# Attention and two expert layers on one core: q and k turned and summed in one product, batch 0's v summed on the tensor engine, and a new table of places

## The chip, the cores and the metric

One NeuronCore of a Trainium2 chip runs the whole kernel. The metric is the device time of one execution in microseconds (us), the median of several runs. The engines are PE (TensorE, matmul; its weight loads are listed as PEld), DVE (VectorE), ACT (ScalarE), POOL (GpSimd) and SP (SyncE, which issues every transfer of this kernel). They run side by side, each takes its instructions strictly in the order of the program, and semaphores make one wait for another.

## What is computed

```python
# q, k, v: (4 batches, 8 heads, 576 tokens, 64);  D = 64, factor = 4
q_d, k_d, v_d = (mean of 4 neighbouring tokens of q, k, v)
out_d = softmax(q_d @ k_d.T / sqrt(D)) @ v_d            # 144 x 144 per head
out_up = np.repeat(out_d, 4, axis=2)
mask = np.abs(pos[:, None] - pos[None, :]) < 4
out_local = softmax(where(mask, q @ k.T / sqrt(D), -1e9)) @ v
x = (out_up + out_local) as 2304 tokens x 512
for w_in, w_out, a in ((moe, 1.0), (moe2, 1.702)):       # 512 -> 2048 -> 512
    h = x @ w_in;  x = (h / (1 + exp(-a * h))) @ w_out
```

The weights come as 64-bit floats and are taken apart on the chip, as pairs of 32-bit words.

## The kernel before

**Tiling.** The attention is cut into 32 units. Unit u is half a batch (288 tokens, m = u // 4) of two heads (hp = u % 4). Batch 0 is m = 0 and 1, so units 0 to 7; its q and k are loaded with 96 tokens on the partitions and turned on PE. From m = 2 on ("blocked"), q and k are loaded in blocks of 32 and turned on DVE.

**Steps of a unit**, with the names that the text uses:
- KT, KC: PE turns k (`kps<-ident,kraw`, six transposes of 96 columns) and makes the sums of four tokens (`kps<-four,kraw`, six products of 24 columns); ACT copies both out. Once for each batch and pair of heads.
- QT, QC: the same for q, three and three, once a unit.
- KV: POOL adds four tokens of v (two additions of `vraw`, a second load of v, into `vd`). Once for each batch and pair of heads.
- SC: scores on PE (`sl`). DM, LC, LS, LU, RC, LN: maxima, capping, subtraction, sums, reciprocal and normalizing of the softmax, on DVE and in part on POOL. DE, LE, DN: the exponentials and a scaling on ACT (DN on DVE for the units that the list `ON` doesn't name).
- TP, TC: the 144-wide softmax turned on PE and copied by ACT. AV: the products with v (`ul`). UC, XA, XM: the sum of both attentions into `xf`, and its largest value.

**Layer 1.** w_in and w_out come in eight loads of 1 MB each (`ldst1...`, two for each c = 0..3). Each load is converted by ACT (ca, cz), DVE (cs, sg, cp) and PE (sps, sums of magnitudes), then split into two 16-bit halves (hi on ACT, lo on DVE, L377 and L381). `ON` moves single sg, cp and other steps from one engine to another. When the four units of half a batch are done, rm, am and pw find a scale, xh and xl split x, and h1.m.p.i (24 products of L706 a pair) and o1.m... follow. The first products of a layer are h1.0.0.0.

**Layer 2.** Its weights are converted during layer 1, kept in DRAM, and split later (L381 again). Each of nine blocks of 256 tokens takes a scale: before, dx (a maximum of four values on DVE and an identity scaled by it, L766 and L768), rm (L775, a product of 128 columns), am (a maximum of 128).

**The order.** All steps are added to a plan with their dependencies. Each step's place is read from the string `PLACES` (two digits in base 62 a step); `placed` sorts by it and raises an error when a step would stand ahead of one that it depends on. So every engine's order, SP's included, is the order of the table. A list `first` at the end adds soft edges between the early loads; soft edges don't bind the table.

Of the kernel before, what the change touches and what calls it, by code (L numbers as in the profile page):

```python
# [20 lines left out]
SCD = 1.0 / 128.0  # L21

GS1, GS2 = 2.0 ** -15, 2.0 ** -26
BAND = 4
ON = {
# [12 lines left out]
def on(name, usual):  # L38
# [8 lines left out]
    "0007020103080c050q1g0J161T1k060g0Y1y1V090v0B0K0Q0P120e0H100M150T1d040s1e0S1h131l0y1m1p1q1r1s1B0V1C1x1G1F1I211v2328292A2d2C2i2W30353e38"  # L47
    "3m262I3n2N3t3c3K0Z181a1u1j1o1A1H1L1S2x2G2j2l2D2O2M2Z3j3l3q4X4h4r2r3f3k3p3v3s3H402E3z3Q3N4G4i4o5a3A4u4M4E5g505f5E3G4H4V4S5r5v5y5P3U4Z5z"
    "5m5L5X62635l615U6e6o6z6H6F5T6r716X7g797e7p5V6M7B6U7G787j7O4q4v6b6j6g6m5O6i6D766T726V6Z7m7x7s7F7E7K7P847V818R0b0f0a0d0h0i0m0k0r0l0o0t0u"
    "0C0z0D0F0N0X14191b0n0w0x0j0p0A0G0E0L0I0O0R0U110W1c1f171D1J1M251n1t1O1i1w1z1N1E1Q1K1R1X1Y1Z202b2f272g2q2t2w1P1W2o1U22242c2e2h2k2n2p2s2v"  # L50
    "2u2y2B2z2F2H2J2K2P2T2U343a2X2Y3S3J517d7h8u2a2m2R3L2L2Q2S36323b373d3i3r3x3y3D3M3E3P3Y415831393o3B3w3I3C3O3R3T3X3Z484f4a4w4D4J5M45494d4m"
    "4j4p4n4y4A4B4K4F4N4Y5d5i5o5t5u4O4T4W565259575e5j5k5q5w5A5F5x5K5Q5S60656t6x7b7k88aU2V335Y4I3g4t6v55427I695J7J8l6N7A3V444e5G5I5Z6c676l6f"
    "6k6p6u6C6A6G6R7i7l7q7t8H4c5D5s5B5N6B6S6L776Q747f7o7v7z7L857Q868c8k945h5p8b6a6K7H7U7R827Z8f8g8j8o8m8z8C8K8O8T8V8X8h8s8x8q8r8y8E8A8J8F8M"
    "8P8Q8Z8U8Y9192979f9i9k9o9H9Ja2af9VdO708v8e95899e9m9q9s9u9t9A9C9D9S9G9L9Oa6acahakc893989z9M9P9X9ZaaadaAaQaCaFaOaVaZb6bbbTa3a5aqaIaBaKaE"
    "aTaXaYb4b1biblb9bGbKbNbOb3bfbjbnbobsbtbybzbBbDbHbPbSbQbUbWbYc5cmcqcIcLcWecj6au8Daian8natbkb7bwcJbLbpcfe0e3cMbdbEajaSbMc2c4c9cgcbcecjcl"
    "ctcpcscDcHcNcQd0d9cackcdc0c6coczcvcFcxcRcScVdgcXd8dtdodxdBdDeEcrcCdTcwcEdbdjdfdndidkdGdIdRdQdWeje8eneueBeLdwdyegd4d5dFdXdUe2e6elepeseD"
    "eweFeIeHeMeOeQeReWeYflftfDgfhgcyd6effXe9ebeSf3f1f5f8fbfefffgfhfnfqfjfNfTfWgFemerfcfyfmfEfrfHfJfKfLfMg5g9fQgqgwgygOeZfafZgbg2gigcgpgCgU"
    "gVh3hbhihshAhHhJhLgjgmgKhhgNhmgPgShqhrhthIhNhRhOhUhZi3i7injejgjYkgkMkUeqhzgBfFdziRiNgtf9jUjCidgkkhjIjLi2f7fOiIg6gaieigikihiqisiCiGiYiJ"
# [160 lines left out]
def kernel(ctx: ExitStack, tc: tile.TileContext, q, k, v, w1_in, w1_out, w2_in, w2_out, out):  # L219
# [537 lines left out]
    def split(L, n, src, skeys, mkey, mget, T_, rmax):  # L757
# [12 lines left out]
        def a():  # L770
            T["rm" + bk] = bank1("rm") if L.n == 1 else pools["pr"].tile([P, 512], F32, tag="pr", name="rm")
            if L.n == 1:
                nc.tensor.matmul(T["rm" + bk][:, :KC], ones32, mget(), start=True, stop=True)
            else:
                nc.tensor.matmul(T["rm" + bk][:, :P], ones32, T["dg" + bk], start=True, stop=True)  # L775
# [751 lines left out]
```

## Time and profile before

| | us |
|---|---|
| median of 3 runs | 893.99 (892.43 to 894.34) |
| profiled execution, its time | 892.67 |
| profiled execution, its span on the core | 890.9 |
| PE busy in that span | 864.1 (97%) |
| DVE busy | 608.9 (68%) |
| ACT busy | 470.4 (53%) |
| POOL busy | 160.8 (18%) |

The span runs from the first to the last instruction; 1.77 us of the execution's time lie around it. A busy share is a mean over the whole span, so the stretches of the span are to be read one by one. "PEclk" is the TensorE clock that the throttle granted as far as the trace has an event for it; ahead of the first event it shows 1.00.

### The profile page before, as it was taken

To read this page: it belongs to the slowest core of one execution; us is meant where nothing else is said; L and a number is where in the kernel's file an instruction comes from. 1 tells how busy PE (TensorE), PEld (TensorE's weight loads), DVE (VectorE), ACT (ScalarE), POOL (GpSimd) and SP (SyncE) were. 2 spreads that over 40 slices of the span, in tenths; PEclk is the share of its full clock that TensorE was granted. 3 is DMA by queue.
4 is the path that set the end of the run, shared out by engine and by line. 5 is a ranking of instruction groups with operands and counts; after the bars stand their busy time and mean duration, and the time that the engine had idled before them with its cause. 6 is when DMAs were issued, how large, how long until landed. Compare 5 with 4: busy or idle time off the path is not lost.

```text
span 890.9 us, 23880 instructions
## 1 busy us (share of the span) xinstructions
PE 864.1 (97%) x10212; PEld 721.5 (81%) x10212; DVE 608.9 (68%) x1334; ACT 470.4 (53%) x841; POOL 160.8 (18%) x187
## 2 busy tenths in 40 slices
PE   6889899999999999999999999999999999999998
PEld 5767676777777777777777788888888888888887
DVE  2989998766867668576485899484764638465572
ACT  4889884654655556566652855342442525243341
POOL 3113631211311141313120002030031400000000
PEclk9999999999999999999999999999999999999999
DMA  9998744263644365524316310000000000000000
GB/s 241 228 244 226 199 100 86 45 120 67 120 114 117 88 156 140 152 80 135 116 61 248 101 43 1 25 1 24 2 13 1 25 24 1 37 1 25 1 25 24
DMA packets 116190, 77.04 MB, mean 86 GB/s; under 512 B 94836, under 2 KB 101492, under 8 KB 115060
## 3 DMA queue, kind: packets, MB, share of 16 engines
q1 hardware_dynamic: 116084, 75.52, 32.1%
q8 instruction: 80, 1.31, 0.6%
q14 instruction: 26, 0.21, 0.1%
HBM read 62.39 MB, written 13.11 MB: 85 GB/s over the span
## 4 chain that ended last, share of the span: by engine, by line
PE 84%; DVE 11%; ACT 2%; issue 1%; DMA 0%; SPq 0%; DVEq 0%; ACTq 0%
PE ops L823 19%; PE hps L706 18%; PE hps L885 18%; PE oy L964 10%; PE oz L964 5%; PE ox L964 3%; PE ul L1291 2%; PE sl L1209 2%; PE ops L851 2%; DVE g L913 1%; PE sl L1203 1%; PE ul L1285 1%; DVE wout L381 1%; PE tps L1268 1%; PE kps L1134 1%
## 5 line engine op out<-in xcount | busy, mean ns | idle before, releaser
L706 PE MATMUL hps<-xhl,win 128*128 128x288 f16 x1536 | 197.9, 287 | 0.1
L885 PE MATMUL hps<-xhl,win 128*128 128x256 f16 x1728 | 190.4, 273 | 1.3 <-DVE tg L900 1.3
L885 PEld LDWEIGHTS <-win 128*128 128x128 f16 x1728 | 169.1, 98 | 21.2 <-issue 1.6
L706 PEld LDWEIGHTS <-win 128*128 128x128 f16 x1536 | 148.5, 98 | 37.8 <-issue 0.4
L823 PE MATMUL ops<-g,wout 128*128 128x288 f16 x1344 | 171.7, 286 | 0.0
L964 PEld LDWEIGHTS <-g 128*128 128x128 f16 x1512 | 147.7, 98 | 18.6 <-issue 0.8
L823 PEld LDWEIGHTS <-wout 128*128 128x128 f16 x1344 | 129.5, 98 | 32.7 <-issue 0.6
L897 ACT ACTIVATE tg<-hps,blk 128x512 f32<-128x512 f32 x72 | 49.5, 687 | 123.9 <-PE hps L885 111.2
L900 DVE SCALAR_TENSOR_TENSOR tg<-tg,hps 128x512 f32<-128x512 f32 x72 | 49.1, 682 | 53.1 <-ACT tg L897 53.1
L913 DVE SCALAR_TENSOR_TENSOR g<-tg,g 128x896 f16<-128x896 f32 x72 | 78.1, 1097 | 0.6 <-ACT g L910 0.3
L904 POOL TENSOR_TENSOR tg<-tg 128x128 f32<-128x128 f32 x19 | 15.1, 793 | 341.9 <-DVE tg L900 341.9
L910 ACT ACTIVATE g<-tg 128x896 f16<-128x896 f32 x72 | 67.5, 945 | 16.1 <-DVE tg L906 12.0
L964 PE MATMUL oy<-wout,g 128*128 128x256 f16 x648 | 75.1, 272 | 0.0
L349 POOL TENSOR_TENSOR cs<-cs,cz 128x512 int32<-128x512 int32 x32 | 43.9, 1378 | 149.0 <-DVE cs L332 67.7
L718 ACT ACTIVATE tg<-hps,blk 128x576 f32<-128x576 f32 x64 | 47.0, 734 | 34.4 <-PE hps L706 27.7
L721 DVE SCALAR_TENSOR_TENSOR tg<-tg,hps 128x576 f32<-128x576 f32 x64 | 47.6, 744 | 18.8 <-ACT tg L718 18.8
L942 ACT ACTIVATE o<-oy,blk 128x256 f32<-128x256 f32 x27 | 12.7, 472 | 76.8 <-PE oy L964 76.8
L731 DVE SCALAR_TENSOR_TENSOR g<-tg,gs,g 128x576 f16<-128x576 f32 x56 | 46.4, 839 | 9.7 <-ACT g L728 9.7
L728 ACT ACTIVATE g<-tg,gs 128x576 f16<-128x576 f32 x56 | 42.7, 769 | 14.6 <-DVE tg L721 14.6
L948 DVE SCALAR_TENSOR_TENSOR o<-oy,blk,o 128x256 f32<-128x256 f32 x9 | 4.4, 484 | 55.4 <-PE oy L964 55.4
L324 ACT ACTIVATE st<-st 128x512 f32<-128x512 f32 (+1 forms) x48 | 39.5, 827 | 2.0 <-DMA st<-in_moe_w_out_dram 2.0
L1239 ACT ACTIVATE pd<-sl,nm 72x144 f32<-72x144 f32 x64 | 23.4, 369 | 16.3 <-DVE nm L1219 12.0
(169 smaller groups left out, 1197.7 us busy)
## 6 DMA issues: line engine op xcount, KB each, us to landing
st<-in_moe_w_in_dram SPq DMA_DIRECT2D x8, 1024.0 KB
st<-in_moe_w_out_dram SPq DMA_DIRECT2D x8, 1024.0 KB
st<-in_moe_w_in_dram SPq DMA_DIRECT2D x16, 512.0 KB
st<-in_moe_w_out_dram SPq DMA_DIRECT2D x16, 512.0 KB
vw<-in_v_dram SPq DMA_DIRECT2D x62, 96.0 KB
vraw<-in_v_dram SPq DMA_DIRECT2D x16, 288.0 KB
out_dram<-o SPq DMA_DIRECT2D x18, 256.0 KB
wdin<-cs SPq DMA_DIRECT2D x16, 256.0 KB
```

Source lines behind the costliest of these rows:

```text
L349: eng.tensor_tensor(out=s, in0=s, in1=zget(), op=ALU.add)
L706: nc.tensor.matmul(o, T[w][:, kc, a, fc * P:(fc + 1) * P], T[xk][:, kc, b, :T_], start=(n == 0), stop=(n == 3 * KC - 1))
L718: ACT.activation(out=T[tg], in_=T[ps][:, :, :T_], func=AF.Tanh, scale=T["a" + bk][:, c:c + 1])
L721: DVE.scalar_tensor_tensor(out=T[tg], in0=T[tg], scalar=1.0, in1=T[ps][:, :, :T_], op0=ALU.add, op1=ALU.mult)
L731: DVE.scalar_tensor_tensor(out=T[g][:, 1], in0=T[tg], scalar=gs, in1=T[g][:, 0], op0=ALU.mult, op1=ALU.subtract)
L823: nc.tensor.matmul(o, w[:, j, a, dc * P:(dc + 1) * P], g[:, b, j % 2, :], start=(n == 0), stop=(n == 3 * NF - 1))
L885: nc.tensor.matmul(o, T[w][:, kc, a, fc * P:(fc + 1) * P], T[xk][:, kc, b, :], start=(n == 0), stop=(n == 3 * KC - 1))
L897: ACT.activation(out=four(), in_=T[ps][:, 0, :], func=AF.Tanh, scale=T["a" + bk][:, c:c + 1])
L900: DVE.scalar_tensor_tensor(out=four(), in0=four(), scalar=1.0, in1=T[ps][:, 0, :], op0=ALU.add, op1=ALU.mult)
L910: ACT.activation(out=T[g][:, 0], in_=T[tg], func=AF.Copy, scale=GS2)
L913: DVE.scalar_tensor_tensor(out=T[g][:, 1], in0=T[tg], scalar=GS2, in1=T[g][:, 0], op0=ALU.mult, op1=ALU.subtract)
L964: nc.tensor.matmul(T[bank[acc]], g[:, a, slot, :], w, start=first and p == p0 and i == 0, stop=prod in (2, 3, 4) and p == NF // 2 - 1 and ...
```

## The change

1. `four` now holds [sums of 4 | identity | sums of 4 over 128] side by side. KT becomes six products of 120 columns, QT three, with no transpose. The copies out take the same number of elements, in another pattern, and the scores of units 0 to 7 read q in another pattern.
2. For batch 0 the second load of v (`vraw`, 4 x 288 KB) and KV on POOL go. In their place VP on PE makes the sums from `vw`, the v that AV loads anyway: six products with a 0/1 matrix `vsum`, 72 weight columns, 128 moving columns. VC on ACT copies 256 columns out.
3. In layer 2 dx goes; rm multiplies the four maxima directly (4 columns), and am takes a maximum of 4.
4. GS2, a power of two by which layer 2's g is scaled, is 2^-19 and was 2^-26.
5. The list `first` goes, `ON` changes, and `PLACES` is a new table for all steps.

```diff
-GS1, GS2 = 2.0 ** -15, 2.0 ** -26
+GS1, GS2 = 2.0 ** -15, 2.0 ** -19
...
-    "POOL": ("cp1.out.0.0 cp1.out.0.2 cp1.out.1.0 cp1.out.1.2 cp1.out.2.0 cp1.out.2.2 cp1.out.3.2"),
+    "POOL": ("cp1.out.0.0 cp1.out.0.2 cp1.out.1.0 cp1.out.1.2 cp1.out.2.0 cp1.out.2.2 cp1.out.3.0 cp1.out.3.2"),
...
-        if L.n == 2:
-            add("dx" + bk, "DVE", 0.45, z, r=mkey + sc2, w=["dg" + bk], alloc=[("dgx", "dg" + bk)])
-            mkey = ["dg" + bk]
...
+        for e in range(3):
+            DVE.tensor_reduce(out=T["vsum"][:, e, QB * e:QB * (e + 1)].rearrange("p (i t) -> p i t", i=4),
...
+        DVE.tensor_copy(out=T["four"][:, QB:QB + TT], in_=T["ident"][:, :TT])
+        DVE.tensor_reduce(out=T["four"][:, :QB], in_=T["ident"][:, :TT].rearrange("p (t r) -> p t r", r=BAND), axis=AX.X, op=ALU.add)
+        DVE.tensor_scalar(out=T["four"][:, QB + TT:], in0=T["four"][:, :QB], scalar1=SCD, scalar2=None, op0=ALU.mult)
...
-                nc.tensor.transpose(T[kps][:, c // NBL, (c % NBL) * TT:(c % NBL + 1) * TT], kr[:, c], T["ident"][:TT, :TT])
-            for c in range(2 * NBL):
-                nc.tensor.matmul(T[kps][:, c // NBL, HALF + (c % NBL) * QB:HALF + (c % NBL + 1) * QB], kr[:, c], T["four"][:TT, 0], start=True, stop=True)
+                nc.tensor.matmul(T[kps][:, c // NBL, (c % NBL) * (QB + TT):(c % NBL + 1) * (QB + TT)], kr[:, c], T["four"][:TT, :QB + TT],
+                                 start=True, stop=True)
...
+            for c in range(2):
+                for e in range(3):
+                    nc.tensor.matmul(o[:, c], T["vsum"][:, e], vw[:, c, e], start=e == 0, stop=e == 2)
...
+        if b:
+            add("KV" + nm, "POOL", 2.1, sv, r=["vraw" + nm], w=[vd], alloc=[("vd", vd)])
+        else:
+            add("VP" + nm, "PE", 1.3, vsum, r=["vw" + nm, "cap"], w=[vps], alloc=[("pa1", vps, hp + 0.45)])
+            add("VC" + nm, "ACT", act(4 * D), vcp, r=[vps], w=[vd], alloc=[("vd", vd)])
...
-    first = []
-    for hp, p in zip(range(NHP), ("0.0", "0.2", "1.0", "1.2")):
-        first += [f"lk0.{hp}", f"lqqraw{hp}", f"vw0.{hp}", f"lv0.{hp}", "ldst1in." + p]
...
```

**PE, from its first instruction.** Before, the order is KT and QT of unit 0, SC0, QT1, KT of the second pair of heads, SC1, TP0. The numbers behind the names tell one buffer from another.

```order
L1132 MATMUL kps_200<-ident_135,kraw_171 128x96 x6
L1134 MATMUL kps_200<-four_168,kraw_171 128x24 x6
L1177 MATMUL qps_215<-ident_135,qraw_174 128x96 x3
L1179 MATMUL qps_215<-four_168,qraw_174 128x24 x3
L1203 MATMUL sl_233<-kd_225,qT0_160 72x144 x2
L1209 MATMUL sl_233<-kT0_148,qT0_160 32x32 x24
L1177 MATMUL qps_260<-ident_135,qraw_179 128x96 x3
L1179 MATMUL qps_260<-four_168,qraw_179 128x24 x3
L1132 MATMUL kps_274<-ident_135,kraw_192 128x96 x6
L1134 MATMUL kps_274<-four_168,kraw_192 128x24 x6
L1203 MATMUL sl_310<-kd_301,qT1_161 72x144 x2
```

The same stretch of PE in the changed kernel:

```order
L1191 MATMUL qps_204<-four_170,qraw_171 128x5x24 x3
L1127 MATMUL kps_209<-four_170,kraw_177 128x120 x6
L1191 MATMUL qps_220<-four_170,qraw_180 128x5x24 x3
L1215 MATMUL sl_232<-kd_225,qT0_160 72x144 x2
L1222 MATMUL sl_232<-kT0_148,qT0_160 32x32 x24
L1127 MATMUL kps_265<-four_170,kraw_174 128x120 x6
L1166 MATMUL vps_291<-vw_183,vsum_168 72x2x64 x6
L1215 MATMUL sl_309<-kd_299,qT1_161 72x144 x2
```

QT1 now stands first, QT0 behind KT, and VP of the first pair of heads between the second KT and SC1. The other three VP stand between QT2 and TP1, between the fourth KT and TP2, and between the last sps of load 2.2 and TP3, so all four ahead of AV3.

**SP, from its first transfer.** Before:

```order
L1065 DMA vraw_169<-in_v_dram 72x4x256
L1053 DMA kraw_171<-in_k_dram 96x6x64 x2
L1053 DMA qraw_174<-in_q_dram 96x3x64 x2
L522 DMA st2_177<-in_moe_w_in_dram 128x2x1024
L1053 DMA qraw_179<-in_q_dram 96x3x64 x2
L1053 DMA kraw_192<-in_k_dram 96x6x64 x2
L522 DMA st2_195<-in_moe_w_in_dram 128x2x1024
```

In the changed kernel:

```order
L1047 DMA qraw_171<-in_q_dram 96x3x64 x2
L1047 DMA kraw_174<-in_k_dram 96x6x64 x2
L1047 DMA kraw_177<-in_k_dram 96x6x64 x2
L1047 DMA qraw_180<-in_q_dram 96x3x64 x2
L521 DMA st2_197<-in_moe_w_in_dram 128x2x1024
L1093 DMA vw_183<-in_v_dram 32x11x64
```

The load of `vraw` that stood first is gone, q of unit 1 stands first, and the k that PE needs first (`kraw_177`) is the third load.

**DVE, behind its set-up.** Before, from the first scores on:

```order
L1224 TENSOR_TENSOR sc<-sl,cap 128x192
L1227 TENSOR_REDUCE mx<-sc 128x6
L1233 TENSOR_TENSOR sc<-sc,mx 128x192
L1217 TENSOR_REDUCE nm<-sl 72x2
L1246 TENSOR_REDUCE smr_164<-sc 128x6
L1250 TENSOR_SCALAR smr_164<-smr_164 128x8
L1251 RECIPROCAL smr_164<-smr_164 128x8
```

In the changed kernel:

```order
L331 TENSOR_SCALAR x_80<-st_197 128x1024
L1230 TENSOR_REDUCE nm<-sl 72x2
L1237 TENSOR_TENSOR sc<-sl,cap 128x192
L1240 TENSOR_REDUCE mx<-sc 128x6
L1259 TENSOR_REDUCE smr_164<-sc 128x6
L1263 TENSOR_SCALAR smr_164<-smr_164 128x8
L1264 RECIPROCAL smr_164<-smr_164 128x8
L1274 TENSOR_TENSOR sc<-sc,smr_164 128x192
L1271 TENSOR_TENSOR pd<-pd,smr_164 72x288
```

The first conversion of a weight load (L331) stands ahead of the first scores, LS0 (L1233) has gone to POOL, and LN0 and DN0 (the last two rows) have come to DVE.

## Rows read from the trace of the kernel before

**Rows 1.** The page, part 1: busy time of each engine.

```profile
PE 864.1 (97%) x10212; PEld 721.5 (81%) x10212; DVE 608.9 (68%) x1334; ACT 470.4 (53%) x841; POOL 160.8 (18%) x187
```

**Rows 2.** Stretches: length, busy us of the engines, PEclk, DMA share, GB/s.

```profile
6.00:25.00 19.00, 16.04 (x178) 14.46 (x178) 5.69 (x15) 10.40 (x24) 4.43 (x5) 1.00 1.05 283
25.00:55.40 30.40, 25.67 (x428) 22.35 (x426) 27.04 (x62) 24.15 (x44) 5.44 (x6) 1.00 1.02 223
55.40:67.00 11.60, 10.47 (x102) 8.47 (x104) 11.32 (x27) 11.07 (x17) 0.89 (x1) 1.00 1.01 244
67.00:105.00 38.00, 36.53 (x688) 28.99 (x687) 36.66 (x98) 36.38 (x66) 20.09 (x16) 1.00 0.77 218
105.00:111.50 6.50, 3.24 (x75) 2.34 (x73) 6.36 (x16) 4.82 (x8) 2.38 (x1) 1.00 1.00 176
111.50:114.90 3.40, 3.40 (x16) 2.15 (x15) 3.30 (x12) 3.40 (x6) 0.51 (x1) 0.50 0.53 92
...
143.00:500.00 357.00, 356.86 (x4888) 281.06 (x4887) 247.15 (x619) 202.77 (x441) 75.94 (x70) 1.00 0.44 116
500.00:550.00 50.00, 48.74 (x417) 40.55 (x415) 47.83 (x58) 31.85 (x36) 5.21 (x8) 1.00 0.13 43
```

**Rows 3.** Waits of PE until 143 us: total us, times, longest.

```profile
PE kps L1132 <- DMA kraw<-in_k_dram: 6.1, 1, 6.1
```

**Rows 4.** Chain that ended last, the first units: start, us, what.

```profile
6.12 1.20 PE kps L1132 x6
7.32 2.44 PE kps L1134 x12
9.76 0.55 PE qps L1177 x3
10.30 1.17 PE qps L1179 x6
...
15.34 1.03 PE kps L1132 x6
16.37 2.45 PE kps L1134 x12
...
19.81 0.76 PE sl L1203 x4
```

**Rows 5.** The same chain, later: AV3, the first products of layer 1.

```profile
53.76 0.75 PE ul L1285 x8
...
63.96 2.88 PE hps L706 x12
...
68.53 1.47 PE hps L706 x12
```

**Rows 6.** The same chain, layer 2's rm, 128 columns, two passes.

```profile
477.20 0.22 PE rm L775 x2
```

**Rows 7.** DVE in order of time: start, us, last what ended the idle.

```profile
21.30 0.36 DVE L1224 TENSOR_TENSOR sc<-sl,cap 128x192 f32<-128x192 f32 x1 [3.98 <-PE sl L1209]
41.21 1.82 DVE L381 SCALAR_TENSOR_TENSOR win<-x,bin,win 128x1024 f16<-128x1024 f32 x1 [0.37 <-ACT win L377]
44.04 1.22 DVE L349 CUSTOM_DVE_ANT_0 x<-x,z 128x2048 uint16<-128x2048 uint16 x1
57.44 1.28 DVE L381 SCALAR_TENSOR_TENSOR win<-x,bin,win 128x1024 f16<-128x1024 f32 x1
105.92 2.35 DVE L1250 TENSOR_SCALAR smr<-smr 128x8 f32<-128x8 f32 x1
121.60 0.16 DVE L1250 TENSOR_SCALAR smr<-smr 128x8 f32<-128x8 f32 x1
```

**Rows 8.** POOL in order of time, the same places.

```profile
41.22 0.72 POOL L1154 TENSOR_TENSOR vd<-vraw 72x256 f32<-72x256 f32 x1
105.86 2.38 POOL L349 TENSOR_TENSOR x<-x,z 128x1024 int32<-128x1024 int32 x1 [4.71 <-PE spo L576]
```

**Rows 9.** DVE groups in layer 2, dx: busy us, mean ns, idle.

```profile
L768 DVE TENSOR_SCALAR dgx<-ident,blk 128x128 f32<-128x128 f32 x9 | 2.6, 287 | 0.4
```

More of the change, by code (lines that the diff above doesn't have):

```diff
@@ L762, in split @@
         bank = ("pa1", "rm" + bk, 4 * n + 3.9) if L.n == 1 else ("pr", "rm" + bk)
-        def z():
-            DVE.tensor_reduce(out=small(L, n, 7), in_=mget(), axis=AX.X, op=ALU.max)
-            T["dg" + bk] = pools["dgx"].tile([P, P], F32, tag="dgx", name="dgx")
-            DVE.tensor_scalar(out=T["dg" + bk], in0=T["ident"], scalar1=small(L, n, 7), scalar2=None, op0=ALU.mult)
         def a():
             T["rm" + bk] = bank1("rm") if L.n == 1 else pools["pr"].tile([P, 512], F32, tag="pr", name="rm")
[L772 to L775, printed above, removed]
+            nc.tensor.matmul(T["rm" + bk][:, :KC], ones32, mget(), start=True, stop=True)
         def b():
             T["am" + bk] = small(L, n, 8)
-            DVE.tensor_reduce(out=T["am" + bk], in_=T["rm" + bk][:, :KC if L.n == 1 else P], axis=AX.X, op=ALU.max)
+            DVE.tensor_reduce(out=T["am" + bk], in_=T["rm" + bk][:, :KC], axis=AX.X, op=ALU.max)
         def d():
@@ L793, in split @@
         sc2 = ["scope2"] if L.n == 2 else []
-        if L.n == 2:
-            add("dx" + bk, "DVE", 0.45, z, r=mkey + sc2, w=["dg" + bk], alloc=[("dgx", "dg" + bk)])
-            mkey = ["dg" + bk]
         add("rm" + bk, "PE", 0.2, a, r=mkey + sc2, w=["rm" + bk], alloc=[bank])
-        add("am" + bk, "DVE", 0.16 if L.n == 1 else 0.28, b, r=["rm" + bk], w=["am" + bk])
+        add("am" + bk, "DVE", 0.16, b, r=["rm" + bk], w=["am" + bk])
         add("pw" + bk, "DVE", 0.5, d, r=["am" + bk], w=[("inv", bk)])
@@ L1025, in attention_init @@
             POOL.memset(t, 1.0)
-        T["four"] = ac.tile([P, 2, QB], F32, name="four")
+        T["vsum"] = ac.tile([P, 3, PD], F32, name="vsum")
+        POOL.memset(T["vsum"], 0.0)
+        T["four"] = ac.tile([P, TT + 2 * QB], F32, name="four")
     def init_cap():
         cap = T["cap"]
-        DVE.tensor_reduce(out=T["four"][:, 0], in_=T["ident"][:, :TT].rearrange("p (t r) -> p t r", r=BAND), axis=AX.X, op=ALU.add)
-        DVE.tensor_scalar(out=T["four"][:, 1], in0=T["four"][:, 0], scalar1=SCD, scalar2=None, op0=ALU.mult)
+        for e in range(3):
+            DVE.tensor_reduce(out=T["vsum"][:, e, QB * e:QB * (e + 1)].rearrange("p (i t) -> p i t", i=4),
+                              in_=T["ident"].rearrange("p (i j) -> p i j", i=4)[:, :, BAND:BAND + QB].rearrange("p i (t r) -> p i t r", r=BAND),
+                              axis=AX.X, op=ALU.add)
+        DVE.tensor_copy(out=T["four"][:, QB:QB + TT], in_=T["ident"][:, :TT])
+        DVE.tensor_reduce(out=T["four"][:, :QB], in_=T["ident"][:, :TT].rearrange("p (t r) -> p t r", r=BAND), axis=AX.X, op=ALU.add)
+        DVE.tensor_scalar(out=T["four"][:, QB + TT:], in0=T["four"][:, :QB], scalar1=SCD, scalar2=None, op0=ALU.mult)
         for i in range(4):
@@ L1131, in tr @@
             for c in range(2 * NBL):
[L1132 to L1134 removed]
+                nc.tensor.matmul(T[kps][:, c // NBL, (c % NBL) * (QB + TT):(c % NBL + 1) * (QB + TT)], kr[:, c], T["four"][:TT, :QB + TT],
+                                 start=True, stop=True)
         def cpy():
[L1137 removed]
+            kp = T[kps][:, :, :NBL * (QB + TT)].rearrange("p c (e t) -> p c e t", e=NBL)
+            ACT.copy(out=T["kTs"][hp][:, BAND:BAND + S].rearrange("p (c e t) -> p c e t", c=2, e=NBL), in_=kp[:, :, :, QB:])
             T[kd] = pools["at"].tile([P, 2 * PD], F32, tag="kd", name="kd", bufs=NHP)
[L1139 removed]
+            ACT.copy(out=T[kd].rearrange("p (c e t) -> p c e t", c=2, e=NBL), in_=kp[:, :, :, :QB])
         def turn():
@@ L1162, in keys_of, with vsum, vcp @@
             add("KD" + nm, "DVE", dve(S), pool, r=[kT], w=[kd], alloc=[("kd", kd)])
-        add("KV" + nm, "POOL", 2.1, sv, r=["vraw" + nm], w=[vd], alloc=[("vd", vd)])
+        vps = "vps" + nm
+        def vsum():
+            T[vps] = bank1("vps")
+            o = T[vps][:PD, :4 * D].rearrange("p (h c d) -> p c h d", h=2, c=2)
+            vw = T["vw" + nm].rearrange("p (h c e) d -> p c e h d", h=2, c=2)
+            for c in range(2):
+                for e in range(3):
+                    nc.tensor.matmul(o[:, c], T["vsum"][:, e], vw[:, c, e], start=e == 0, stop=e == 2)
+        def vcp():
+            T[vd] = pools["at"].tile([PD, 4, D], F32, tag="vd", name="vd", bufs=NHP)
+            ACT.copy(out=T[vd].rearrange("p j d -> p (j d)"), in_=T[vps][:PD, :4 * D])
+        if b:
+            add("KV" + nm, "POOL", 2.1, sv, r=["vraw" + nm], w=[vd], alloc=[("vd", vd)])
+        else:
+            add("VP" + nm, "PE", 1.3, vsum, r=["vw" + nm, "cap"], w=[vps], alloc=[("pa1", vps, hp + 0.45)])
+            add("VC" + nm, "ACT", act(4 * D), vcp, r=[vps], w=[vd], alloc=[("vd", vd)])
     def unit(u):
@@ L1175, in qtr @@
             T[qps] = bank1("qps")
+            o = T[qps][:, :HALF + PD].rearrange("p (i c t) -> p c i t", i=5, c=NBL)
             for c in range(NBL):
-                nc.tensor.transpose(T[qps][:, c * TT:(c + 1) * TT], T[f"qraw{u}"][:TT, c * 2 * D:(c + 1) * 2 * D], T["ident"][:TT, :TT])
-            for c in range(NBL):
-                nc.tensor.matmul(T[qps][:, HALF + c * QB:HALF + (c + 1) * QB], T[f"qraw{u}"][:TT, c * 2 * D:(c + 1) * 2 * D], T["four"][:TT, 1], start=True, stop=True)
+                nc.tensor.matmul(o[:, c], T[f"qraw{u}"][:TT, c * 2 * D:(c + 1) * 2 * D], T["four"][:TT, QB:], start=True, stop=True)
         def qcp():
@@ L1474 @@
             s.deps.setdefault(s3, False)
-    by = {s.name: s for s in plan.steps}
-    first = []
-    for hp, p in zip(range(NHP), ("0.0", "0.2", "1.0", "1.2")):
-        first += [f"lk0.{hp}", f"lqqraw{hp}", f"vw0.{hp}", f"lv0.{hp}", "ldst1in." + p]
-    first += ["ldst1in." + p for p in ("2.0", "2.2", "3.0", "3.2")]
-    for c in range(NC):
-        first += [f"ldst1out.{c}.0", f"lqqraw{NHP + c}", f"ldst1out.{c}.2"]
-    for a, b in zip(first, first[1:]):
-        plan.soft.append((by[a], by[b]))
     order = plan.placed(PLACES)
```

90 lines of the change are left out of this document (44 added, 46 removed), and 15 rows, old and new, of the table ON.

## The prediction

> **What bounds the kernel now.** I read the shares first [rows 1]: PE is busy 97% of the span, so a gain must be PE time that is idle, slow or superfluous. The stretches [rows 2] say where that is. From 143 to 500 us PE has no idle time to speak of (356.86 of 357.00), from 500 to 550 it lacks 1.26. Everything else is lost ahead of 143 us: PE starts at 6.12, when the first k has landed [rows 3, 4], it then idles 2.96 of the 19.0 us to 25, 4.73 of the next 30.4, 1.13 of the next 11.6, 1.47 to 105, and 3.26 of 6.5 us around 108. It is slow too: the first twelve products of layer 1 take 2.88 us, the next twelve 1.47 [rows 5]. So PE stands at the lower of its two levels (1.2 GHz) until about 67 us and at the higher (2.4 GHz) behind it; the column of the granted clock reads 1.00 there only because no event lies ahead. After the stop around 108 it reads 0.50 for 3.4 us [rows 2], which costs 1.7 us.
>
> What makes PE wait is mostly DVE. It is nearly idle at first (5.69 of 19.0 us until 25), then busy 27.04 of 30.4, 11.32 of 11.6, 36.66 of 38.0 and 6.36 of 6.5 [rows 2]: from the second unit's scores at 21.3 on it works through the weights' conversions and the attention almost without a break. It waited 3.98 us for those scores [rows 7]. So the time is set by when DVE's run begins and by how much work it holds; PE's own work counts where DVE, ACT and PE wait for each other, until AV3 at 53.76 [rows 5].
>
> **The change part by part.** Durations are of the execution of 892.67 us, which lies 1.32 us below the median of the three runs (893.99).
>
> *Products of 120 columns.* At the lower level six transposes take 1.03 us and the six products of 24 columns 2.45, in two passes each: 0.204 us a pass [rows 4]. With so few columns it is the load of 128 weight columns that sets a pass. A pass of 128 columns over 128 weight columns takes 0.11 at the higher level [rows 6], 0.22 at the lower. So a pass of 120 lies between 0.204 (all columns hidden behind the weight load) and 0.22; I take 0.204, and the six transposes fall away: 1.03 us for each KT, 0.55 for each QT. If 0.22 is right, a KT saves 0.84. ACT's copies keep their size. The other pattern of q is read by PE alone and costs nothing.
>
> *VP.* Six products of 128 columns in two passes are twelve passes. Between 12 x 0.22 = 2.64 us by the row of 128 columns [rows 6] and 12 x 0.38 = 4.56 by the scores' products, which take 0.76 for two passes one behind the other with 72 weight columns and 144 moving ones [rows 4]. I take 2.64, since VP uses all 128 rows like rm, where the scores' two halves share the array. It lies ahead of AV3 four times: 10.6 us of new PE work at the lower level, against 4 x 1.03 + 4 x 0.55 = 6.3 saved. VC adds four copies on ACT of 256 columns.
>
> *The first scores.* How SC1's end, 21.26 before [rows 4, 7], moves: PE's first k is the third load instead of the second, 144 KB more ahead of it (720 KB, not 576), at 283 GB/s [rows 2] +0.5. KT and QT of unit 0 are 1.03 + 0.55 shorter. QT1 (0.55 + 1.17) leaves the chain, since it now runs while k is still landing. The second KT is 1.03 shorter. VP adds 2.64, but hides the wait for the copy of kd ahead of SC1 (0.99 from 18.82 to 19.81). Sum: 0.5 - 1.58 - 1.72 - 1.03 + 2.64 - 0.99 = -2.2 us. DVE's run begins that much earlier.
>
> *From SC1 to AV3.* PE gets 3 x 2.64 = 7.9 more and 2 x (1.03 + 0.55) = 3.2 less, 4.7 in all. It idled 4.73 in 25 to 55.4 and about 1 more between SC1 and 25 [rows 2], together as much as that. What stands behind a VP on PE is a TP or SC1, and behind these the softmax copies and AV. As DVE's list holds conversions between these steps, I take it that the idle time covers the 4.7; without the cover AV3 comes 2.5 us later than before instead of 2.2 earlier.
>
> *DVE's own work.* KV goes from POOL, and with it a disturbance: a split (L381) that began beside POOL's addition at 41.2 took 1.82 us where others take 1.28 [rows 7, 8]. One such place, -0.5. The changed lists give DVE two DN and exchange LS and LN, which nearly cancels: +0.2. One conversion (cp1.out.3.0) moves from DVE, 1.22 us [rows 7], to POOL, 2.38 [rows 8]. But POOL can hold up DVE: a tiny operation of 0.16 us took 2.35 when it began just behind POOL's L349 [rows 7, 8]. So this edit is worth between -1.2 and 2.2 - 1.2 = +1.0; I take -1.2, because only one of the two cases shown here stands at such a place and the table puts all these steps elsewhere.
>
> The Trainium skill ("SBUF — State Buffer", the section on shared ports) says that the pair of SBUF ports shared by DVE and GpSimd is an exclusive lock held for a whole instruction, and that the loser waits entirely. The row of 2.35 us agrees with it. By that rule each conversion given to POOL threatens one stall of up to 2.2, and the sum below would be 2.2 worse.
>
> *Loads.* 4 x 288 KB less stand ahead of the weights: 1.18 MB at 223 GB/s [rows 2] is 5.3 us of transfers. Hidden in my sum: from 25 us on DVE has work, so earlier weights don't start it earlier. Without that cover (DVE waiting for weights) up to 5 us.
>
> *Layer 2.* dx (0.29 us and a small maximum, nine times [rows 9]) leaves DVE, where PE never waits but for the 1.26 us in 500 to 550 [rows 2]. I take 0, bounds -1.3 and +1.3, since the order there is new too. rm keeps two loads of 128 weight columns, so PE saves nothing. GS2 only scales: 0. QT4 to QT7 save PE 0.55 each at the lower level or half of it at the higher, where DVE sets the pace: 0, bound -1.6 (two and two).
>
> **Sum.** -2.2 - 0.5 + 0.2 - 1.2 = -3.7: 892.67 - 3.7 = **889.0 us**.
>
> **The rivals.**
> *A, forecast*, DVE's run begins 2 us earlier and is 1.5 shorter: 889.0, chance 0.44, its own range 886.5 to 891.5.
>
> *B, the clock rises earlier.* PE was busy 25.67 of the 30.4 us until 55.4 [rows 2], much of it with transposes and 24-column products, and still stood at the lower level at 63.96 [rows 5]. The new KT, QT and VP keep the columns streaming in nearly every pass. If this raises the clock at some 20 us, PE's work until 64 halves, at most 18 us, but DVE caps the gain at the 3.6 us that it idles from 25 to 67 [rows 2], and the first twelve products of layer 1 give 1.4 [rows 5]: 889.0 - 5.0 = 884.0. Against it: AV3 and the sps that follow leave gaps in which it may fall again. Chance 0.20.
> The Trainium skill ("TensorE: Matmul & The Clock Gate", on PE-mode transposes) says that transposes don't count as a busy PE for the clock. By that rule B happens; no row separates the transposes from the small products.
>
> *C, slower: VP is dear.* If each pass costs 0.38, VP takes 4.56. SC1 is then 0.3 later than my sum only by -2.2 + 1.9, and until AV3 PE gets 3 x 4.56 - 3.2 = 10.5 more, of which 5.7 find idle time: AV3 comes 4.5 later than before, DVE waits for it, 892.67 + 4.5 - 1.5 = 895.7, with a POOL stall 897.9, in the middle 896.8. AV3 comes later than before once a VP costs above 3.4 us, and above 3.8 that outweighs the 1.5. Chance 0.18.
>
> *D, no change.* DVE's run begins earlier, but the wait of PE for DVE around 108 comes back larger, as the order is new, with one POOL stall (2.2) and order losses of the same size as the 1.5: 892 to 893.5. Chance 0.18.
>
> **How the numbers follow.** The predicted time is A's. The range takes in B and its bound below (884.0 less 1.6 for the QTs and 1.3 for layer 2, so 881) and most of C above (897). 0.2% (1.8 us, so 892.2 and 895.8) is about what a measurement of this kernel can tell from no change. Faster: A, B and a third of D, 0.70. Same: the rest of D and a little of C, 0.14. Slower: 0.16.
>
> **What would show it.** Right: PE's first k product near 6.5 us; twelve passes of 120 columns in 2.4 to 2.7 us; SC1's end near 19; VP at 2.6; L706 at its faster rate from about 65; PE idle before 143 us smaller by 3 to 4. B would show in products of the early stretch at half their time. C in VP above 3.4 us and AV3 behind 55. D in small DVE operations of 2 us beside POOL's L349 and a stop of PE ahead of layer 1's second product. I am wrong if SC1 doesn't come earlier, or if the weights' landing, not DVE, sets the early pace: then up to 5 us more is gained.

## The result, and the profile after

The changed kernel takes 884.92 us (median, 884.48 to 885.38), the one before in the same runs 894.16: 9.2 us less, a ratio of 0.9907, interval 0.9887 to 0.9928. It is faster, and by more than the 3.7 us of the forecast. The profiled executions, 0.3 us above the one median and 1.5 below the other, take 885.25 and 892.67, so 7.4 us less; what follows accounts for these 7.4.

The stretches of the changed kernel, as in [rows 2] (us, PE, PEld, DVE, ACT and POOL busy, granted clock, DMA share, GB/s):

```profile
0.00:6.00 6.00, 1.61 (x6) 1.35 (x6) 2.06 (x12) 0.00 (x0) 2.58 (x25) 1.00 0.66 139
6.00:25.00 19.00, 16.14 (x235) 14.29 (x235) 8.23 (x22) 13.50 (x26) 0.51 (x1) 1.00 0.98 278
25.00:55.40 30.40, 22.70 (x383) 20.55 (x383) 27.24 (x64) 25.98 (x46) 3.75 (x4) 0.73 0.95 266
55.40:67.00 11.60, 11.05 (x173) 8.86 (x172) 10.94 (x30) 10.70 (x23) 1.02 (x2) 0.67 0.83 235
67.00:105.00 38.00, 34.05 (x643) 26.91 (x643) 37.44 (x88) 34.80 (x59) 17.37 (x12) 1.00 0.69 170
105.00:111.50 6.50, 6.33 (x96) 5.06 (x86) 6.33 (x17) 6.43 (x10) 2.64 (x2) 1.00 0.71 150
500.00:550.00 50.00, 49.97 (x435) 42.19 (x433) 47.53 (x56) 31.22 (x34) 9.86 (x12) 1.00 0.12 43
```

PE starts earlier (QT1 in 0 to 6), it no longer stops in 105 to 111.5 (6.33 of 6.50, before 3.24), and the 1.26 us that it lacked in 500 to 550 are gone. In 67 to 105 it is idle for longer (3.95 us, before 1.47). PE in order of time, the part that answers to [rows 4]:

```profile
4.39 1.63 PE L1191 MATMUL qps<-four,qraw 96*128 96x120 f32 x6 [4.39 <-DVE four L1025]
7.00 2.89 PE L1127 MATMUL kps<-four,kraw 96*128 96x120 f32 x12 [0.97 <-DMA kraw<-in_k_dram]
...
13.18 2.91 PE L1127 MATMUL kps<-four,kraw 96*128 96x120 f32 x12
15.88 2.77 PE L1166 MATMUL vps<-vw,vsum 128*72 128x128 f32 x12
18.58 0.50 PE L1215 MATMUL sl<-kd,qT 64*72 64x144 f32 x4
...
23.03 1.60 PE L1127 MATMUL kps<-four,kraw 96*128 96x120 f32 x12 [0.38 <-DVE xf L1319]
```

From start to start the twelve passes of k take 2.70 us (13.18 to 15.88) and those of VP also 2.70 (to 18.58): 0.225 a pass each. The same twelve passes take 1.60 at 23.03: PE is at its higher level there, which before it reached only at 67 us. The clock column shows how long this lasts:

```profile
18.70:32.30 13.60, 9.93 (x267) 8.29 (x267) 10.97 (x25) 10.94 (x22) 0.00 (x0) 1.00 0.97 249
32.40:42.50 10.10, 8.80 (x60) 8.29 (x59) 9.38 (x22) 9.09 (x17) 2.73 (x2) 0.50 1.07 316
```

DVE's run, to be held against [rows 7], and POOL beside it:

```profile
19.68 0.36 DVE L1237 TENSOR_TENSOR sc<-sl,cap 128x192 f32<-128x192 f32 x1 [2.38 <-PE sl L1222]
...
78.17 2.53 DVE L1263 TENSOR_SCALAR smr<-smr 128x8 f32<-128x8 f32 x1
...
95.41 1.86 DVE L459 TENSOR_TENSOR prod<-wsm,ibin 128x1 f32<-128x1 f32 x1
...
121.46 1.86 DVE L459 TENSOR_TENSOR prod<-wsm,ibin 128x1 f32<-128x1 f32 x1
```

```profile
78.31 2.36 POOL L348 TENSOR_TENSOR x<-x,z 128x1024 int32<-128x1024 int32 x1
...
94.58 2.67 POOL L348 TENSOR_TENSOR x<-x,z 128x1024 int32<-128x1024 int32 x1 [1.29 <-ACT z L344]
...
120.46 2.84 POOL L348 TENSOR_TENSOR x<-x,z 128x1024 int32<-128x1024 int32 x1 [0.76 <-ACT z L344]
```

The first scores of unit 1 come to DVE at 19.68 instead of 21.30. The stalls of small DVE operations beside POOL's conversion have not gone. There are three, at other places than before (elsewhere L1263 takes 0.17 us and L459 0.14), and PE stops behind each, for 1.55, 1.86 and 1.31 us:

```profile
83.30 0.93 PE L1191 MATMUL qps<-four,qraw 96*128 96x120 f32 x6 [1.55 <-DVE xf L1318]
97.83 0.62 PE L575 MATMUL spo<-x,ones 128*128 128x128 bf16 x8 [1.86 <-DVE xf L1318]
105.64 6.05 PE L838 MATMUL ops<-g,wout 128*128 128x288 f16 x48 [0.17 <-DVE tg L720]
124.10 4.16 PE L838 MATMUL ops<-g,wout 128*128 128x288 f16 x19 [1.31 <-DVE x L852]
```

The first output product of layer 1 (`ops`, 105.64) stood at 110.57 before, so 4.9 of the 7.4 us are won by there.

### The profile page after: what moved, and what is told of

It is laid out like the page before. It is cut to its first block, busy times and chain, and to the rows that moved or that the text cites. A ratio compares the mean times of both kernels' runs of the same rounds, so it can differ in the third digit from the quotient of the medians.

```text
span 883.5 us, 23809 instructions
## 1 busy us (share of the span) xinstructions
PE 858.6 (97%) x10212; PEld 717.4 (81%) x10212; DVE 604.7 (68%) x1319; ACT 467.2 (53%) x833; POOL 154.7 (18%) x187
## 3 DMA queue, kind: packets, MB, share of 16 engines
q8 instruction: 80, 1.31, 0.6%
## 4 chain that ended last, share of the span: by engine, by line
PE 85%; DVE 8%; ACT 3%; DMA 2%; issue 1%; SPq 0%; DVEq 0%; ACTq 0%
PE hps L872 20%; PE ops L810 19%; PE hps L705 18%; PE oy L951 11%; PE oz L951 5%; PE ox L951 2%; PE ul L1304 2%; PE sl L1222 2%; PE ops L838 1%; PE sl L1215 1%; PE ul L1298 1%; PE tps L1281 1%; DMA qraw<-in_q_dram 1%; DVE wout L380 1%; DVE g L900 1%
## 5 line engine op out<-in xcount | busy, mean ns | idle before, releaser
L730 DVE SCALAR_TENSOR_TENSOR g<-tg,gs,g 128x576 f16<-128x576 f32 x56 | 48.6, 873 | 5.7 <-ACT g L727 5.4
L1246 POOL TENSOR_TENSOR sc<-sc,mx 128x192 f32<-128x192 f32 x21 | 12.5, 593 | 121.3 <-DVE mx L1240 121.3
```

What stands on the lines that cost most here:

```text
L730: DVE.scalar_tensor_tensor(out=T[g][:, 1], in0=T[tg], scalar=gs, in1=T[g][:, 0], op0=ALU.mult, op1=ALU.subtract)
```

## The experiments

Twelve kernels, each against the kernel before on the same chip; names in a_ are edits of the changed kernel, in b_ of the kernel before. The kernel before took 893.87, 892.56 and 894.13 us in the three groups of four. The changed kernel was not run again in them, so a distance to its 884.92 is taken across groups; by the ratios to the kernel before it can come out about 1 us otherwise (a_transposes 4.0 above it instead of 3.6, a_cp30_dve 0.4 below instead of 0.6 above).

**Products alone, both ways.** The k part of the edit of a_transposes (q alike, 3 and 3; the scores read q in its former pattern); b_products has the change's own lines in the kernel before.

```diff
-                nc.tensor.matmul(T[kps][:, ... (QB + TT) ...], kr[:, c], T["four"][:TT, :QB + TT], ...)
+                nc.tensor.transpose(T[kps][:, ... TT ...], kr[:, c], T["ident"][:TT, :TT])
+            for c in range(2 * NBL):
+                nc.tensor.matmul(T[kps][:, ... HALF + QB ...], kr[:, c], T["four"][:TT, :QB], ...)
```

> The changed kernel with k's and q's transposes and sums apart again (six transposes and six products of 24 columns for a k, three and three for a q), in the same order and with the same places of all steps. Theory work (the forecast's A): each KT is 0.8 us longer and QT0 0.4, so the first scores of unit 1 come about 2.0 us later, DVE's run begins 2.0 us later, and the time is about 886.9. Theory clock (the forecast's B): the rise of the granted clock at 18.7 us does not come, the products until 63 us stand at the lower level, the first product of layer 1 is slow: 889 to 890. Theory order (the gain is the new order behind 67 us alone, which waits for something else): within 0.8 us of the changed kernel.

> The kernel before with k's and q's transposes and sums in one product of 120 columns, nothing else, same order. Theory work: KT0, QT0, QT1 and KT1 shorten by 0.8 + 0.4 + 0.4 + 0.8 = 2.4 us ahead of unit 1's scores, time 894.2 - 2.4 = 891.8. Theory clock: the clock rises near 20 us and the first products of layer 1 are fast: 889 to 890. Theory order: the stop of PE around 108 us (behind the DVE operation of 2.35 us beside POOL) takes what is gained: 893.4 to 894.8.

Measured: a_transposes 888.57 (0.9952 of before, 0.9934 to 0.9970), 3.6 above the changed kernel. That is more than theory work's 2.0 and lies in none of the three theories: where the products' worth beyond 2.0 comes from in the new order is open. b_products 891.37 (0.9978, 0.9968 to 0.9989), 2.5 below before, as theory work says. The rise of the clock does not come from these products: in b_products the passes stay at the lower level,

```profile
38.87 2.92 PE L1133 MATMUL kps<-four,kraw 96*128 96x120 f32 x12
...
61.70 3.02 PE L706 MATMUL hps<-xhl,win 128*128 128x288 f16 x12
```

and in a_transposes, with transposes but with VP, the scores behind the first VP are at the higher one:

```profile
17.70 2.81 PE L1166 MATMUL vps<-vw,vsum 128*72 128x128 f32 x12
20.84 0.62 PE L1223 MATMUL sl<-kT,qT 64*32 64x32 f32 x48
```

**No dx in layer 2.**

```diff
         def z():
-            DVE.tensor_reduce(out=small(L, n, 7), in_=mget(), axis=AX.X, op=ALU.max)
-            T["dg" + bk] = ...
-            DVE.tensor_scalar(out=T["dg" + bk], in0=T["ident"], scalar1=small(L, n, 7), ...)
+            pass
```

> The kernel before with the step dx of layer 2 left out (rm sums the four columns of the maxima themselves), same order. If the step dx is what PE waits 1.3 us for in 500 to 550 us of the kernel before: 892.9. If that wait belongs to the order (what stood ahead on DVE): 894.2, and the wait is still there. The forecast took 0.

Measured: 893.21 (0.9995, 0.9984 to 1.0006), no difference that can be told. The wait is still there,

```profile
500.00:550.00 50.00, 48.73 (x417) 40.57 (x416) 47.69 (x56) 31.65 (x35) 5.36 (x8) 1.00 0.13 43
```

so dx alone does not carry it; what is left is the order of the table, by elimination. But rm became shorter; the records of its two passes, before and in b_no_dx:

```profile
L775 PE MATMUL rm<-dgx,ones x18: 272/275/275, 477.0 to 791.0; 128*128 128x128 f32 x18
```

```profile
L769 PE MATMUL rm<-blk,ones x18: 169/212/253, 477.0 to 790.3; 128*128 128x4 f32 x18
```

Added up over PE's list without overlaps, all rm take 3.81 us before and 2.88 here: 0.9 us of PE's own time.

**v's sums: on POOL, nowhere, or transposes in their place.** In all three the steps keep their places.

```diff
 # a_kv: VP's step makes the two additions on POOL, VC nothing; vraw is loaded ahead of vw
-            add("VP" + nm, "PE", 1.3, vsum, ...)
+            add("VP" + nm, "PE", 1.3, sv, ...)
 # a_no_vp: vsum does nothing, VC copies four rows of vw
 # a_fill_tr
-                    nc.tensor.matmul(o[:, c], T["vsum"][:, e], vw[:, c, e], start=e == 0, stop=e == 2)
+            for c in range(16):
+                nc.tensor.transpose(T[vps][:, ...], T["ident"][:TT], T["ident"][:TT, :TT])
```

> The changed kernel with the sums of v on POOL from vraw again, loaded just ahead of each unit's vw, instead of the six products on PE and the copy on ACT; all other steps in their places. Theory work: PE has 2.7 us less ahead of unit 1's scores, so DVE's run begins up to 2.7 us earlier, but the loads of 288 KB stand ahead of the weights again: between 882.3 and 886. Theory clock with VP as its carrier: without these products, which keep the columns streaming, the rise at 18.7 us does not come: 887 to 890. If the unit's AV waits for the additions on POOL (2 x 0.72 us and the load): AV0 later than 20.5 and time above 886.

> The changed kernel with VP's six products left out of all four units of batch 0; VC copies four rows of vw instead, so that ACT's work and all waits but PE's stay (the output lacks the sums of v). Theory work: PE has 2.7 us less ahead of unit 1's scores and 8 us less until AV3, so the kernel is up to 2.7 us faster than the changed one: 882.2 to 884.9. Theory clock: VP is what raised the granted clock at 18.7 us; without it the clock stays at the lower level until some 63 us, as it did with v's sums on POOL, and the kernel with less work is slower: 886.5 to 888.

> The changed kernel with 16 transposes of the unit matrix (some 2.75 us at the lower level) in the place of VP's six products of 128 columns; the same bank, copy and order (the output lacks the sums of v). Theory kind (transposes don't raise the clock, as the Trainium skill's page on the clock gate, TensorE: Matmul & The Clock Gate, says in its part on transposes): the clock stays at the lower level until some 63 us, time 888 to 890. Theory busy (any pass without a gap raises it): the rise at 18.7 us is there, and the time within 0.8 us of the changed kernel's 884.9.

Measured: a_kv 887.93 (0.9941, 0.9925 to 0.9956), 3.0 above the changed kernel; a_no_vp 884.06 (0.9900, 0.9882 to 0.9917), not told from it; a_fill_tr 886.34 (0.9926, 0.9911 to 0.9941). So four VP, 9.0 us of PE's list, cost nothing that the times resolve, and v's sums on POOL, with the loads that they need, cost 3 in this order. DVE in a_kv, and POOL, show where:

```profile
28.32 2.29 DVE L380 SCALAR_TENSOR_TENSOR win<-x,bin,win 128x1024 f16<-128x1024 f32 x1
...
39.24 1.17 DVE L1265 TENSOR_TENSOR pd<-pd,smr 72x288 f32<-72x288 f32 x1
...
42.63 0.38 DVE L1283 STREAM_TRANSPOSE PT<-sc 128x192 f32<-128x192 f32 x1 [1.09 <-POOL sc L1268]
...
48.36 1.80 DVE L348 CUSTOM_DVE_ANT_0 x<-x,z 128x2048 uint16<-128x2048 uint16 x1
```

```profile
27.61 1.91 POOL L1151 TENSOR_TENSOR vraw<-vraw 72x512 f32<-72x512 f32 x1 [10.41 <-DMA vraw<-in_v_dram]
...
38.80 1.29 POOL L1151 TENSOR_TENSOR vraw<-vraw 72x512 f32<-72x512 f32 x1 [3.90 <-DMA vraw<-in_v_dram]
...
47.17 1.90 POOL L1151 TENSOR_TENSOR vraw<-vraw 72x512 f32<-72x512 f32 x1
```

The three DVE operations that begin beside POOL's additions take 2.29, 1.17 and 1.80 us; in a_no_vp the same ones take 1.28, 0.46 and 1.21. That is 2.3 us, the longer wait for POOL's LN another 0.7, and rm of layer 1 comes 3.4 us later (56.41 against 53.00). DVE waits for no load there. The time lies in theory clock's range as well, and no product ahead of 64 us is at the higher level in this profile, but DVE's 3.0 us account for it without the clock. AV0 stood at 19.90, so it did not wait for the additions.

Without VP, SC1 waits for the copy of kd, 1.00 us, as the forecast's 0.99 had it. The first products of layer 1 come 1.75 us earlier than in the changed kernel (63.32), also at the higher rate, and the third k is slow where the q behind it is fast:

```profile
16.94 0.76 PE L1210 MATMUL sl<-kd,qT 64*72 64x144 f32 x4 [1.00 <-ACT kd L1134]
...
22.90 2.85 PE L1127 MATMUL kps<-four,kraw 96*128 96x120 f32 x12
...
26.16 0.88 PE L1186 MATMUL qps<-four,qraw 96*128 96x120 f32 x6
...
61.57 1.64 PE L705 MATMUL hps<-xhl,win 128*128 128x288 f16 x12
```

So the level rises without VP too, at 25.6 us, and theory clock, which had it low until 63, falls; at 29.24 it is low again (scores in 0.74 us). The time lies in theory work's range. The lead of 1.75 us is gone by the first output product (105.91 against 105.64).

With transposes in VP's place PE is as busy, but the third k, at 24.31, is still slow; the next filling is fast:

```profile
24.31 2.85 PE L1127 MATMUL kps<-four,kraw 96*128 96x120 f32 x12
...
28.57 1.48 PE L1163 MATMUL vps<-ident 96*128 96x96 f32 x16
```

So the level rose here too, at about 27.8 us: 9 us later than with VP (18.7), and no earlier than with nothing in VP's place (25.6). That is between the two theories. The Trainium skill ("TensorE: Matmul & The Clock Gate", on PE-mode transposes) has it that transposes don't count as a busy PE for the clock. This run agrees with that, since 16 of them brought the rise no earlier than nothing did; it doesn't settle it, since k's products and the sps stand between.

**All edits of code in the order of before.** b_vp has VP alone, b_all all of 1 to 3 of the change; in both VP stands behind TP of its unit. In b_all2 it stands behind the next KT, and vw of units 1 to 3 is loaded in vraw's place.

```diff
 # b_vp, b_all: in dtr, behind TP's transposes
+            if u < NHP:
+                T["vsums" + nm][0]()
 # b_all2: in tr, behind KT's products
+            if b == 0 and hp:
+                T[f"vsums0.{hp - 1}"][0]()
```

> The kernel before with v's sums of batch 0 by VP's six products behind each unit's transposes of pd, and no vraw loads and no additions on POOL in batch 0; all else and the order as before. Theory work (the forecast's price): 4 x 2.7 us of PE work at the lower level, half of it in idle time, less 0.5 on DVE: 895 to 898. Theory clock: VP raises the granted clock before 63 us here too: 889 to 892. Loads alone (1.18 MB less ahead of the weights) and no change of the clock: 892 to 894.

> The kernel before with the products of 120 columns, VP in place of the sums on POOL, and no dx, in the order of before: all edits of code but the new table of places, the lists and the loads' order. If the edits of code make the gain: 884.5 to 887. If the new order makes half of it (its VP stands ahead of unit 1's scores, and the stop around 108 us is gone): 888 to 890. If the parts that were tried alone add up without the clock (2.5 for the products, 0.5 for dx): 891.

> Again all edits of code without the new table of places and lists, as in b_all, but VP of a unit stands behind the next unit's k product (as in the changed kernel) instead of behind its transposes of pd, and vw of units 1 to 3 is loaded where vraw was loaded, so that VP need not wait for it (it waited 5.8 us in b_vp). Theory edits (the code's edits give the gain, once VP's data are there): 885 to 887. Theory order (the gain behind 67 us, the stop around 108 us above all, needs the new order): the products' 2.5 us are kept, VP is hidden, 890 to 892. If VP's work is not hidden in this order: above 893.

Measured: 903.52 (1.0121, 1.0102 to 1.0140), 900.40 (1.0082, 1.0064 to 1.0101) and 897.82 (1.0044, 1.0031 to 1.0056): all slower than before, b_vp and b_all beyond what any theory named, b_all2 as its last one had it. The longest wait of PE behind 7 us is a new one, first in b_vp (in order of time), then in b_all2 (by what PE waited for):

```profile
36.31 2.81 PE L1172 MATMUL vps<-vw,vsum 128*72 128x128 f32 x12 [5.82 <-DMA vw<-in_v_dram]
```

```profile
PE vps L1172 <- DMA vw<-in_v_dram: 6.2, 1, 6.2
```

In the old order vw of a unit lands just ahead of its AV. VP asks for it earlier, and everything behind VP on PE waits with it. In b_all2 the first unit's vw, which I had left at its place, did the same ahead of SC1. These waits are 5.8, 5.5 and 6.2 us, and the kernels lost 11.0, 7.8 and 3.7 against before, so in the first two they are not the whole. The clock did rise early in b_vp (at 24.82 eight sps products take 0.62 us; they take 1.01 at the lower level), and it is the slowest all the same. So these three don't price the order behind 67 us, as I meant them to. They show that VP at these places waits for its data. That the new order of the loads is what mends it is argued and not shown.

**The stop at 108.** cp1.out.2.2 goes from POOL to DVE.

```diff
-    "POOL": ("cp1.out.0.0 ... cp1.out.2.0 cp1.out.2.2 cp1.out.3.2"),
+    "POOL": ("cp1.out.0.0 ... cp1.out.2.0 cp1.out.3.2"),
```

> The kernel before with the POOL conversion of 2.38 us that begins at 105.86 us (cp1.out.2.2), beside which a DVE operation of 0.16 us took 2.35, moved to DVE (1.22 us). If that stall is what stops PE around 108 us and drops its clock: DVE is 2.2 - 1.2 = 1.0 us ahead, the stop is 1 to 2 us shorter, 892 to 893 against 893.9. If the stop is DVE's amount of work and not this stall: within 0.5 us of before, or slower by up to 1.2.

Measured: 891.62 (0.9971, 0.9960 to 0.9981), 2.5 faster, more than I expected. The operation of 2.35 us [rows 7] takes 0.16, the conversion's 1.22 us come behind what PE waits for, and PE's next output product starts at 108.30 instead of 110.57:

```profile
105.85 0.16 DVE L1250 TENSOR_SCALAR smr<-smr 128x8 f32<-128x8 f32 x1
...
108.17 1.22 DVE L349 CUSTOM_DVE_ANT_0 x<-x,z 128x2048 uint16<-128x2048 uint16 x1
```

```profile
107.22 0.62 PE L1268 MATMUL tps<-ident,pd 72*72 72x72 f32 x4 [0.61 <-ACT pd L1256]
108.30 5.87 PE L851 MATMUL ops<-g,wout 128*128 128x288 f16 x33 [0.46 <-DVE tg L721]
```

PE's products behind it stay slow (33 in 5.87 us, where the changed kernel takes 4.57 for 36 at 111.99), so the 2.5 us are those of the stall and not of the clock.

**cp1.out.3.0 on DVE again** (the name taken out of the POOL list of the changed kernel), and **PE's gap ahead of rm filled**:

```diff
+            if bk == "1.0":
+                for _ in range(5):
+                    nc.tensor.matmul(T["rm" + bk][:, P:2 * P], ones32, T["ident"], start=True, stop=True)
             nc.tensor.matmul(T["rm" + bk][:, :KC], ones32, mget(), start=True, stop=True)
```

> The changed kernel with the conversion cp1.out.3.0 on DVE again, at its place in the order. By the forecast's term, 1.2 us on a DVE that sets the pace: 886.1. If POOL's port holds up DVE there as much as it saves: 884.9. If nothing waits for DVE at that place (behind 105 us): 884.9, with no DVE operation of 2 us gone.

> The changed kernel with five products of 128 x 128 of constants (10 passes, some 2.25 us at the lower level) ahead of layer 1's first rm, in the 2.5 us in which PE waits there for DVE; their result is not read. If an unbroken PE keeps the granted clock up from 49.4 us and the clock is what counts: the products until 63 us run at the higher level, 882 to 884. If DVE sets the pace there whatever the clock: 884.5 to 885.5, with the first product of layer 1 at most 1 us earlier. If the clock falls anyway: 885 to 887.

Measured: a_cp30_dve 885.56 (0.9902, 0.9886 to 0.9918), a_fill_rm 886.02 (0.9909, 0.9894 to 0.9924); neither is told from the changed kernel. In the profiles a_cp30_dve is 1.4 us longer (span 884.9 against 883.5), near the forecast's 1.2, but the times don't bear that out. This conversion stands behind the first output product in both kernels (on POOL at 117.33, before on DVE at 121.92), so it has no part in what is won ahead of that product. The filling missed its gap. It began when the gap was nearly over, ran slowly and pushed rm back:

```profile
54.10 2.50 PE L767 MATMUL rm<-ident,ones 128*128 128x128 f32 x10 [1.04 <-DVE xf L1321]
56.39 0.43 PE L768 MATMUL rm<-blk,ones 128*128 128x4 f32 x2
```

So it says nothing on what a steady clock would be worth there.

## Why the forecast was right in sign and short in size

**Where it was right.** The first k at 7.00 (forecast 6.5), the passes at 0.225 us (0.204 taken, 0.22 named as the other end), VP at 2.70 (2.64), the wait for kd that VP hides (1.00 for 0.99). DVE's run begins 1.6 us earlier. The forecast's 2.2 lost some 0.4 to the later k and 0.25 at each KT, which saves 0.8 (3.48 in [rows 4], 2.70 now) and not 1.03; SC1 itself, at the higher level, gave back 0.4 (18.58 to 19.64, before 1.45). *From SC1 to AV3* held: without all four VP AV3 stands at 49.41, with them at 50.32, before at 53.76, so it is 3.4 us earlier where the forecast had 2.2. Nearly all of VP's 9.0 us lie in idle time or are given back by the clock; which of the two, no run tells. The products, tried alone in the kernel before, are worth 2.5.

**The number.** The 884.92 lie inside the whole range but outside A's own (886.5 to 891.5), and nearest to B's 884.0. That nearness is luck, since B's reckoning is not what the runs show (below). One sign failed: PE's idle time before 143 us was to be 3 to 4 us smaller, and it is 0.7 smaller (20.9 us, before 21.6). So little of the gain before 143 us is PE's idle time that closed; its work got shorter.

**The term that came out short** is *DVE's own work*: 1.5 us for the stretch from DVE's first scores of unit 1 to the first output product, which measured 3.3. That stretch, before and after:

```profile
21.30:110.57 89.27, 77.45 (x1299) 63.34 (x1300) 83.75 (x203) 78.57 (x138) 30.05 (x25) 1.00 0.91 224
```

```profile
19.68:105.64 85.96, 72.35 (x1300) 60.14 (x1300) 81.08 (x192) 76.06 (x135) 22.78 (x18) 0.86 0.81 215
```

Two things were left out of it. One is the stop around 108. The section on bounds read it (3.26 of 6.5 us, 1.7 for the clock), *DVE's own work* read the stall behind it, and rival D let it come back larger; the sum left it as it was. Taking POOL's conversion away from that one DVE operation alone is worth 2.5 us in the order of before. But in the new order it can't be the whole of the 3.3: until the first output product PE idles 19.6 us in both kernels, as the stops of 1.55 and 1.86 behind two new stalls came in place of the one at 108.

The other is the table itself. The sum priced steps that change engine, not steps that the table moves. DVE has 203 operations (83.75 us) in this stretch before and 192 (81.08) now, although its stalls there grew from 2.7 to 4.1 us over their plain durations. Without the stalls that is 81.0 and 77.0: 4.0 us less work ahead of the product. A turn of k with its sum (1.5 us) now stands behind it, and one conversion (0.7) and steps of a softmax stand ahead of the first scores. PE's own work in the stretch fell as well, from 77.45 to 72.35 us; that DVE's list and not PE's sets the length is argued from a_no_vp, where PE has four VP less and the first output product comes no earlier.

**Layer 2** was taken as 0 within 1.3 either way. It gave 2.2: the wait of 1.3 is gone, by elimination through the order and not through dx, and "PE saves nothing" at rm was wrong by 0.9. Together: 1.6 + 3.3 + 1.3 + 0.9 = 7.1 of the 7.4 us. The rest isn't placed. Before had a second stall with a stop of PE of 2.06 us behind it (L460 took 2.13 at 127.13), which the forecast did not read; the changed kernel has one of 1.31 instead (124.10), and the steps moved behind the first output product count against this. The spell at the lower clock is in both kernels, before behind 110.57 and now behind 124.10. The further 1.8 us by which the medians differ lie in no profile here.

**KV.** The 0.5 was read from where KV stood before and was never tried alone. In the changed kernel's order the additions with their loads cost 3.0 (a_kv), so the forecast's price can hold at most for the old places.

**The small terms.** GS2 was not tried alone. The -1.2 for cp1.out.3.0 is neither confirmed nor refuted by the times, and it stands behind the stretch of the 3.3.

**The rivals.** B's event came: the clock rises at 18.7 us, and the first twelve products of layer 1 take 1.64 us (3.08 before in the same list), its 1.4. Its cause is open. The rise follows VP here and in a_transposes, but comes without VP in a_no_vp at 25.6, and it does not come early with the products of 120 columns alone (b_products) or behind b_all's first VP. Nor is B's whole 5.0 shown: the kernel without VP, with less work on PE and the later rise, is not told from the changed one. C fell (0.225 a pass, not 0.38). D's sign came three times, small DVE operations of 2 us beside POOL's conversion with stops of PE of 1.55, 1.86 and 1.31, but not at 108, and the time that D gave did not follow. What stays open is how the 3.3 us divide between the loads' order, the stalls' places, the steps that moved and the clock, since no kernel had the new order with the old code, and mine with the new code in the old order ran into the loads.

## What to carry to other kernels

A stop that is seen in the profile is a term of the sum: if a change reorders that place, price the stop's end as well as its return. A new table also moves work past the product that ends a stretch: count what the engine that sets the pace has to do in the stretch, before and after, and not only the steps that change engine. A stall of a small DVE operation beside a long POOL one is cheap to try, by moving that one POOL operation, and in the order of before it was worth as much as the whole edit of q's and k's products. Work that is moved to an engine with idle time needs its data earlier than the work that it replaces: look at when they land before pricing the instructions.

## What was not expected

VP's products of 72 weight columns and 128 rows take 0.225 us a pass, the same as k's of 128 weight columns, 96 rows and 120 columns. The start differs between kernels that are alike up to there: the changed kernel has its AV0 at 20.49, a_fill_rm, with the same instructions until 51 us, at 21.96, with SC1's end at 19.64 and 20.97. In a_fill_rm the first VP waited 0.97 us for vw, and the clock rose at about 20.9 us instead of 18.7. At AV3 they are 1.1 us apart, and the times are not told apart.
